# Attention with a mixture of experts behind it: blank rows written as fixed heads of the experts' regions, an expert's last tile placed to end with its tokens, and a smaller descriptor scratch

## The chip, the cores and the metric

One core of a Trainium2 chip. The metric is the device time of one execution in microseconds, the median of several runs.

## The reference

```python
def _attn_ref(q, k, v, w1, b1, w2):            # 8 batches, 8 heads, 576 rows, head_dim 64
    scores = scale * q @ k.T + bias            # bias from a small MLP of relative positions
    attn = softmax(scores)
    return attn @ v

def _moe_ref(x, modality_id, w_gate, modality_bias, w1, w2):   # x: 4608 tokens of 512
    logits = x @ w_gate + modality_bias[modality_id]
    e_idx = np.argmax(logits, axis=1)          # one of 8 experts for each token
    gate_w = softmax(logits) at e_idx
    for e in range(E):
        mask = e_idx == e
        h = np.maximum(x[mask] @ w1[e], 0.0)   # 512 -> 1024
        out[mask] = gate_w[mask, None] * (h @ w2[e])
```

## The kernel before

**Attention.** After a table of biases (up to about 66 us) come 32 pairs of heads, four to a batch, about 17 us each. The order of the work of a pair is written out by hand in `ORDER`, five units of letters: S scores, t and T transposes of the exponentials, a and A, b and c the products with V, 0 to 4 the preparation of Q and K of the next pair, W its swap (two DMAs that write the other half of QT, L426 and L427), K its copies of KH and QD, V its load of V, L the loads of Q and K of the pair after that, q and k their split on GpSimd (L384, L388). The letters X and B are places for routing work: each takes the next step from a list of two kinds in `self.bg` (`route_next`; X takes kind 0, B kind 1). X stands in units 0, 2 and 4, B in units 0, 1 and 2. Routing steps exist from the end of pair 4 on, when the first batch is done; before that `bg` is None and the places are empty.

**Routing.** `route_steps` computes, for each batch, the tokens' experts, counts (`base`, the next free row in each expert's region) and positions, and scatters the rows (token, gate, id) with an indirect DMA of GpSimd (L904) into `xg`, a tensor in HBM: 8 regions of `n_tab` = 4864 rows of 516 words, and 32 rows behind them.

**Experts.** Work goes in tiles of TS = 256 rows of one expert. The first K = 5 tiles (`moe_first`) are made of full tiles known after six of the batches; beside them runs the routing of the last batch. Then come the remaining large tiles (`moe_rest`), and up to NT = 3 tiny tiles of NS = 32 rows for remainders. Tables (`first`, `big`, `tiny`; `table`, `last_tables`) say for each tile which expert it has and at which row of `xg` it starts; VectorE makes them on one partition in some thirty short instructions. A tile is `phase1` (x by w1, L1229) and `phase2` (hidden by w2, L1246, two halves). In the middle of `phase2` stand the transposes of the next tile's rows (`xprep`, L1209), so `load_rows` (L1131, a DMA from `xg` into one of two buffers `gx`) must have landed by then; `load_rows(4)` is issued after tile 2, `load_rows(5)` after tile 3. Weights are loaded on condition that the expert is new (`load_new`, L1122 and L1125), and split into a high and a low part by ScalarE (L1191) and VectorE (L1192), one part of w2 between each two groups of `phase1`, and w1 ahead of `phase2`. All these DMAs are issued by SyncE, in the order of the program.

**Blank rows.** An expert's last tile reads past its tokens. So that what it reads there is harmless (zeros, and the id `n_tok`, which the output's scatter leaves out), `fill_steps` writes blank rows: 32 behind the regions (L1147) and, for each expert, 256 rows from where its tokens end (L1157, the row read from `tab_end`). The steps marked F in the list in `moe_first` issue them, in tiles 2 and 3; each letter string of that list is used up by one call of `beside`, six for a tile. All are writes to `xg`, as the scatters are, at rows known only when the kernel runs; so the framework makes each wait for the one before, and the loads of rows wait for them.

Of the kernel before, what the change touches and what calls it, by code (L numbers as in the profile page):

```python
# [11 lines left out]
F32 = mybir.dt.float32  # L12
BF16 = mybir.dt.bfloat16
F32R = mybir.dt.float32r
I32 = mybir.dt.int32
AF = mybir.ActivationFunctionType
ALU = mybir.AluOpType
AX = mybir.AxisListType
# [3 lines left out]
P = 128  # L22
# [7 lines left out]
E = 8  # L30
# [80 lines left out]
class Attn:  # L111
# [501 lines left out]
    def attention(self):  # L613
        n_pair = self.n_pair
        tail = self.first_tiles() if self.K else {}
        for at in self.ROUTE_LATE:
            tail.setdefault(at, []).append(lambda: next(self.route, None))
        for u, k in self.LATE:
            tail.setdefault((0, u), []).append(lambda k=k: next(self.late[k], None))
        bg = None  # L620
        for n in range(n_pair + 1):
            for u in range(5):
                for f in tail.get((n, u), ()):
                    f()
                if u == 4 and n > 0 and n % NP == 0:
                    assert not bg or all(k == len(x) for x, k in bg)
                    bg = self.route_steps(n // NP - 1)
                m, w = (n, u - 2) if u >= 2 else (n - 1, u + 3)
                scored = []
                for op in self.ORDER[u].split():  # L630
                    op, self.defer = op[0], int(op[1:] or 0)
                    if op in "aAbc":
                        self.flush(lambda x: x[0][0] in "er")
                    elif op in "WK" or (op == "S" and u == 0):
                        self.flush(lambda x: x[0][0] == "p")
                    elif op == "X":
                        self.flush(lambda x: x[0][0] == "a")
                    self.held = [] if self.defer and op in "01234tTRAc" else None
                    if op in "SefC":
                        if n == n_pair:  # L640
                            continue
                        if op == "S":
                            scored.append(self.scores(n, 2 * u + len(scored)))
                        elif op == "C":
                            self.compact(n, u)
                        else:
                            self.exps(*scored["ef".index(op)])
                    elif op in "tT":
                        if 0 <= m < n_pair:
                            self.etrans(m, w, "tT".index(op))  # L650
                    elif op in "RaAbc":
                        if n > 0:
                            self.rtrans(n - 1) if op == "R" else self.av(n - 1, *divmod("aAbc".index(op), 2))
                    elif op in "01234WKV":
                        if n + 1 < n_pair:
                            if op in "01234":
                                self.prep(n + 1, int(op))()
                            else:
                                {"W": lambda: self.swap(n + 1), "K": lambda: self.heads(n + 1), "V": lambda: self.load_v(n + 1)}[op]()
                    elif op in "qkL":  # L660
                        if n + 2 < n_pair:
                            self.load_qk(n + 2) if op == "L" else self.split(n + 2, "qk".index(op))
                    elif f := self.route_next(bg, "XB".index(op)):
                        f()
                    fresh, self.held = self.held or [], None
                    for x in self.waiting:
                        x[2] -= 1
                    self.flush(lambda x: x[2] <= 0)
                    self.waiting += fresh
                if 0 <= m < n_pair:  # L670
                    del self.E[m, w]
        self.flush(lambda x: True)
        self.bg = bg


    def route_setup(self, cp):
# [2 lines left out]
        B = self.B  # L679
        NC = 5 * B  # L680
        self.n_tab = -(-self.n_tok // TS) * TS + TS
        self.xg = self.dp.tile([E * self.n_tab + NS, XW], F32, name="xg")

        self.ones = cp.tile([P, P], BF16, name="ones")
        nc.gpsimd.memset(self.ones, 1.0)
# [12 lines left out]
        self.base = cp.tile([P, E], F32, name="base")  # L698
        nc.sync.dma_start(self.base, io["c_ebase"].to_broadcast([P, E]))
        yield  # L700
        self.gi = cp.tile([P, 5, 4], F32, name="gi")
        nc.gpsimd.memset(self.gi, 0.0)
        self.ids = cp.tile([P, NC], F32, name="ids")
# [227 lines left out]
    def moe_early(self, cp):  # L931
# [12 lines left out]
        self.gk = cp.tile([1, E, self.n_kt], F32, name="gk")  # L944
        self.ge = cp.tile([1, n_tt, E], F32, name="ge")
        self.tf = cp.tile([1, 4, n_tt], F32, name="tabf")
        self.ev = {nm: cp.tile([1, E], F32, name=nm) for nm in ("cnt", "off", "cum", "val", "taken", "start", "big")}
        self.pad = [cp.tile([1, 4 + E], F32, name=f"pad{k}") for k in range(3)]
        for t in self.pad:
            nc.vector.memset(t, 0.0)  # L950
# [3 lines left out]
        nc.vector.memset(self.ev["taken"], 0.0)  # L954
        self.tabs = {nm: cp.tile([1, 4, n], I32, name=f"tab_{nm}") for nm, n in (("first", max(1, self.K)), ("big", hi + 1 - self.K), ("tiny", E))}
        self.idt = cp.tile([P, 4], I32, name="idt")
        self.tab_end = cp.tile([1, E], I32, name="tab_end")
        self.ids_q = [cp.tile([P, 1], I32, name=f"idsq{k}") for k in range(NT)]
        self.quad = cp.tile([P, 1], F32, name="quad")
        nc.sync.dma_start(self.quad, self.io["c_quad"])  # L960
# [51 lines left out]
    def table(self, nm, nt, start):  # L1012
# [10 lines left out]
        def s_cum():  # L1023
            self.running()
            V.tensor_tensor(ev["val"], nt, ev["cum"], op=ALU.subtract)
            V.scalar_tensor_tensor(ev["val"], ev["val"], float(TS), start, op0=ALU.mult, op1=ALU.add)
            V.tensor_tensor(ev["val"], ev["val"], self.eb, op=ALU.add)

        def s_expert():
            V.tensor_tensor(ge, col(tt), row(ev["cum"]), op=ALU.is_ge)  # L1030
# [3 lines left out]

        def s_row():
            V.tensor_tensor(ge, col(f[:, 0, :]), row(self.iota), op=ALU.is_equal)
            V.tensor_tensor(ge, ge, row(ev["val"]), op=ALU.mult)
            V.tensor_reduce(f[:, 1, :], ge, axis=AX.X, op=ALU.add)
            V.scalar_tensor_tensor(f[:, 1, :], tt, float(TS), f[:, 1, :], op0=ALU.mult, op1=ALU.add)
            if nm != "tiny":  # L1040
                V.tensor_tensor(f[:, 1, :], f[:, 1, :], f[:, 3, :], op=ALU.mult)
                return

            empty = float(E * self.n_tab)
            V.scalar_tensor_tensor(f[:, 1, :], f[:, 1, :], -empty, f[:, 3, :], op0=ALU.add, op1=ALU.mult)
            V.tensor_scalar(f[:, 1, :], f[:, 1, :], empty, None, op0=ALU.add)
            V.tensor_copy(tab[:, 0:2, :], f[:, 0:2, :])
            V.tensor_copy(tab[:, 3, :], f[:, 3, :])
# [28 lines left out]
    def last_tables(self):  # L1077
# [2 lines left out]

        def s_count():
            V.tensor_tensor(ev["cnt"], self.base[0:1, :], self.eb, op=ALU.subtract)
            V.tensor_copy(self.tab_end, self.base[0:1, :])
            self.counts(ev["big"], NS + 0.5)
            V.tensor_scalar(ev["start"], ev["big"], float(TS), None, op0=ALU.mult)
            V.tensor_tensor(ev["nt"], ev["cnt"], ev["start"], op=ALU.is_gt)
# [49 lines left out]
    def ids_of(self, t):  # L1136
        return [self.idt[:, (2 * t + w) % 4 : (2 * t + w) % 4 + 1] for w in range(2)]

    def fill_steps(self):

        nc = self.nc
        z = self.lt

        def blank():
            nc.gpsimd.memset(z[:, 0:DM], 0.0)
            nc.gpsimd.memset(z[:, DM:XW], float(self.n_tok))
            nc.sync.dma_start(self.xg[E * self.n_tab : E * self.n_tab + NS, :], z[0:NS, :])  # L1147

        def end(e):
            off = nc.values_load(  # L1150
                self.tab_end[0:1, e : e + 1],
                engines=[mybir.EngineType.SP],
                min_val=0,
                max_val=E * self.n_tab - TS,
                skip_runtime_bounds_check_because="an expert's rows end one tile before the next expert's",
            )
            nc.sync.dma_start(  # L1157
                self.xg[ds(off, TS), :].rearrange("(p w) c -> p w c", w=2),
                z.rearrange("p (o c) -> p o c", o=1).to_broadcast([P, 2, XW]),
            )  # L1160

        return [blank] + [lambda e=e: end(e) for e in range(E)]

    def gate(self, t):
        return [self.gates[:, (2 * t + w) % 4 : (2 * t + w) % 4 + 1] for w in range(2)]
# [157 lines left out]
    def route_rest(self):  # L1323
        while any((f := self.route_next(self.bg, kind)) and [f()] for kind in (1, 0)):
            pass
        for f in self.fills:
            f()

    def moe_first(self):


        steps = iter("B,X,X,X,,X,BB,,X,B,B,X,X,X,X,X,BBF,BBFF,BF,BF,BF,BF,BBF,BF".split(","))

        def beside():
            for op in next(steps, ""):
                f = next(self.fills, None) if op == "F" else self.route_next(self.bg, "XB".index(op))
                if f:
                    f()

        self.fills = iter(self.fill_steps())  # L1340
        if self.K > 1:
            self.load_rows(1)
        if self.K:
            self.moe_load(1)
        for t in range(self.K):
            self.tile(t, beside)
        self.route_rest()
# [164 lines left out]
```

## Time and profile before

| | |
|---|---|
| Time, median of 3 runs | 1101.06 us (1100.25 to 1104.41) |
| The profiled execution's own time | 1102.27 us |
| Its span, first to last instruction | 1100.5 us |
| Busy: TensorE, VectorE, ScalarE, GpSimd | 96%, 69%, 59%, 29% |
| TensorE's granted clock, mean | 0.991 |
| DMA | 128.09 MB, mean 116 GB/s |

The span is cut by stage: biases to about 66 us, attention to about 630, the first five tiles to about 790, the other tiles to the end. Busy shares are means over these stages. The chain of waits goes back from the last instruction to what released it, step by step; a stretch that the chain spends away from TensorE is one in which TensorE waited.

### The profile page before, as it was taken

The numbers are of one execution on the slowest core, as the hardware profiler recorded it, in microseconds if no ns is written. First come the engines' busy times: TensorE is split into PE (matmuls) and PEld (weight loads), VectorE is DVE, ScalarE is ACT, GpSimd is POOL, SyncE is SP. The second block draws the span as 40 slices with busy tenths as digits, with TensorE's granted clock in tenths as the row PEclk, the third lists the DMA queues.
The fourth block names the chain that finished last, engine by engine and source line by source line (L and its number), as shares of the span: only waits on it lengthen the run. The fifth ranks groups of instructions, "written<-read, shape, count | busy, mean of one in ns | idle before, by whom it ended". The sixth has DMA issues, their size and how long they took to land.

```text
span 1100.5 us, 23117 instructions
## 1 busy us (share of the span) xinstructions
PE 1060.9 (96%) x8324; PEld 889.9 (81%) x8324; DVE 761.9 (69%) x1665; ACT 647.6 (59%) x1250; POOL 318.9 (29%) x546
## 2 busy tenths in 40 slices
PE   6979999999999999999999999999999999999994
PEld 3458878888787888888887889988999999889894
DVE  7976678787786877877879776774556654555553
ACT  7766766666666667666666664444555545454552
POOL 0003425535435345273452321521101111101010
PEclk9999999999999999999999999999999999999998
DMA  6984444535354444445353710134113811243310
GB/s 170 225 189 98 124 111 102 155 81 159 96 136 123 114 128 118 119 126 126 102 148 94 228 54 29 69 132 154 50 39 115 296 62 56 84 148 118 113 40 22
DMA packets 88764, 128.09 MB, mean 116 GB/s; under 512 B 30752, under 2 KB 55584, under 8 KB 88642
## 3 DMA queue, kind: packets, MB, share of 16 engines
q1 hardware_dynamic: 82626, 107.58, 35.9%
q0 software_dynamic: 5920, 18.95, 4.8%
q8 instruction: 68, 1.11, 0.4%
q14 instruction: 54, 0.44, 0.1%
q10 hardware_dynamic: 96, 0.00, 0.0%
HBM read 135.62 MB, written 23.44 MB: 145 GB/s over the span
## 4 chain that ended last, share of the span: by engine, by line
PE 81%; DMA 7%; POOL 5%; DVE 4%; issue 1%; ACT 1%; SPq 0%; POOLq 0%; ACTq 0%; DVEq 0%
PE p L1246 16%; PE p L1229 16%; PE xps L545 12%; PE sps L453 11%; PE eps L497 7%; PE xps L402 4%; PE xps L539 3%; PE bps L199 3%; DMA xg<-NBm 3%; POOL qs L384 2%; PE xps L1209 1%; PE eps L503 1%; POOL xg L904 1%; DMA NBm<-xTb 1%; DVE Eb L468 1%
## 5 line engine op out<-in xcount | busy, mean ns | idle before, releaser
L482 ACT ACTIVATE Eb<-Eb,mn 128x576 f32<-128x576 f32 x288 | 222.9, 776 | 145.8 <-DVE mn L468 143.8
L453 PE MATMUL sps<-KT,QT 128*128 128x288 f32 x1152 | 204.6, 312 | 3.7 <-DVE mn L468 2.3
L468 DVE CUSTOM_DVE_ANT_0 Eb<-sps,NBm 128x576 f32<-128x576 f32 x256 | 185.6, 753 | 11.3 <-PE sps L453 4.4
L453 PEld LDWEIGHTS sps<-KT,QT 128*128 128x128 f32 x1152 | 162.0, 188 | 9.3 <-issue 2.9
L1229 PE MATMUL p<-QT,w1hi 128*128 128x256 f32 x1136 | 161.0, 284 | 0.0
L1229 PEld LDWEIGHTS p<-QT,w1hi 128*128 128x128 f32 x1136 | 146.9, 191 | 3.8 <-issue 1.8
L1232 DVE SCALAR_TENSOR_TENSOR hl<-p,hh 128x512 fp32r<-128x512 f32 x72 | 49.7, 690 | 144.3 <-ACT hh L1231 144.3
L497 PE MATMUL eps<-idf,Eb 128*128 128x128 f32 x1024 | 143.8, 275 | 0.0
L545 PE MATMUL xps<-eT,vraw 128*64 128x288 f32 x1024 | 141.8, 412 | 0.5 <-DVE KT L340 0.5
L1255 POOL DMA_INDIRECT out<-mo,idt x36 | 40.9, 1136 | 317.1 <-ACT QT L1212 222.0
L487 POOL COPY rem<-Eb 128x128 f32<-128x128 f32 x128 | 36.6, 293 | 317.2 <-ACT Eb L482 316.6
L338 ACT ACTIVATE eT<-eps 128x512 f32<-128x512 f32 x160 | 94.2, 590 | 41.3 <-PE eps L497 41.2
L497 PEld LDWEIGHTS eps<-idf,Eb 128*128 128x128 f32 x1024 | 113.5, 141 | 6.2 <-DVE mn L468 5.0
L1246 PE MATMUL p<-w2hi,hh 128*128 128x512 f32 x288 | 115.0, 399 | 0.0
L1246 PE MATMUL p<-w2hi,hl 128*128 128x512 f32 x288 | 113.0, 392 | 0.0
L1231 ACT ACTIVATE hh<-p 128x512 fp32r<-128x512 f32 x72 | 43.0, 597 | 116.9 <-PE p L1229 112.9
L545 PEld LDWEIGHTS xps<-eT,vraw 128*64 128x64 f32 x1024 | 65.2, 137 | 48.5 <-issue 12.3
L340 DVE COPY xTb<-xps 128x288 f32<-128x288 f32 x64 | 29.3, 457 | 106.7 <-PE xps L545 58.7
L1192 DVE TENSOR_TENSOR w2lo<-NBm,w2hi 128x1024 fp32r<-128x1024 f32 x72 | 88.2, 1225 | 18.7 <-ACT w2hi L1191 18.7
L1229 PE MATMUL p<-QT,w1lo 128*128 128x256 f32 x568 | 91.3, 283 | 0.0
L1192 DVE TENSOR_TENSOR w1lo<-NBm,w1hi 128x1024 fp32r<-128x1024 f32 x72 | 83.2, 1219 | 7.2 <-ACT w1hi L1191 7.2
L340 DVE COPY eT<-eps 128x512 f32<-128x512 f32 x128 | 84.6, 682 | 0.0
(230 smaller groups left out, 1849.1 us busy)
## 6 DMA issues: line engine op xcount, KB each, us to landing
NBm<-moe_w SPq DMA_DIRECT2D x23, 2048.0 KB
NBm<-moe_w SPq DMA_DIRECT2D x44, 1024.0 KB
QT<-QT SPq DMA_DIRECT2D x64, 304.0 KB
NBr<-xg SPq DMA_DIRECT2D x20, 516.0 KB
NBm<-xTb SPq DMA_DIRECT2D x32, 288.0 KB
KH<-KT SPq DMA_DIRECT2D x64, 144.0 KB
qraw<-q SPq DMA_DIRECT2D x32, 256.0 KB
kraw<-k SPq DMA_DIRECT2D x32, 256.0 KB
```

What stands on the lines that cost most here:

```text
L338: self.nc.scalar.activation(out, ps, AF.Copy, scale=scale)
L340: self.nc.vector.tensor_copy(out, ps)
L402: nc.tensor.transpose(pr[:, j, :], xs[:, 4 * (part % 2) + j, :, :].rearrange("p a d -> p (a d)"), self.idr)
L453: nc.tensor.matmul(ps[:, half, :], q, k[:, HS * half : HS * half + HS], start=i == 0, stop=i == len(terms) - 1, skip_group_check=True,)
L468: nc.vector.tensor_tensor_reduce(out=e.rearrange("p (t w) -> p t w", t=2), in0=ps, in1=nb.rearrange("p (t w) -> p t w", t=2), scale=1.0, s ...
L482: self.nc.scalar.activation(e, e, AF.Exp, bias=mn, scale=-1.0, accum_out=sm)
L497: nc.tensor.transpose(ps[:, k, :], e[:, part, P * k : P * k + P], self.idf)
L545: nc.tensor.matmul(ps[o, :], v[:, h, k, :], self.eT[:, h, k, sl], start=half == 1 and k == 0, stop=half == 0 and k == 3, tile_position=(0, ...
L1192: self.nc.vector.tensor_tensor(l, w, h.bitcast(F32), op=ALU.subtract)
L1229: nc.tensor.matmul(ps[:, a, :], w[:, c, fs], x[:, c, :], start=i == 0, stop=i == len(ops) - 1)
L1232: nc.vector.scalar_tensor_tensor(hl[:, sl, :], ps, 0.0, hh[:, sl, :].bitcast(F32), op0=ALU.max, op1=ALU.subtract)
L1246: nc.tensor.matmul(ps, h[:, f, sl], m[:, f, :], start=i == 0, stop=i == len(ops) - 1)
```

## The change

Each region gets a head: its first 256 rows are written blank at a fixed place, before any token is scattered, by nine DMAs (eight regions and one region more, which stands where the 32 rows behind the regions stood). They take the X places of pairs 1 to 3, and their source is a tile of its own, `blank`, filled by GpSimd in `route_setup`. The writes behind the tokens, `tab_end` and the steps F are gone. The tables `big` and `tiny` get a limit for each expert, max(end of its tokens - width, start of its region), and a tile starts at the lesser of its old row and that limit: the last tile of an expert ends with its tokens and computes some rows a second time, with the same result; a region with fewer tokens than a tile reads into its head. The program's scratch for descriptors of GpSimd's DMAs is set to 2048 bytes in each partition, where nothing was set.

```diff
--- before.py
+++ after.py
@@ -622,6 +622,8 @@
             for u in range(5):
                 for f in tail.get((n, u), ()):
                     f()
+                if n == 1 and u == 0:
+                    bg = self.blanks()
                 if u == 4 and n > 0 and n % NP == 0:
                     assert not bg or all(k == len(x) for x, k in bg)
                     bg = self.route_steps(n // NP - 1)
@@ -679,7 +681,7 @@
         B = self.B
         NC = 5 * B
         self.n_tab = -(-self.n_tok // TS) * TS + TS
-        self.xg = self.dp.tile([E * self.n_tab + NS, XW], F32, name="xg")
+        self.xg = self.dp.tile([(E + 1) * self.n_tab, XW], F32, name="xg")
 
         self.ones = cp.tile([P, P], BF16, name="ones")
         nc.gpsimd.memset(self.ones, 1.0)
@@ -698,6 +700,10 @@
         self.base = cp.tile([P, E], F32, name="base")
         nc.sync.dma_start(self.base, io["c_ebase"].to_broadcast([P, E]))
         yield
+        blank = cp.tile([P, 2, XW], F32, name="blank")
+        nc.gpsimd.memset(blank[:, :, 0:DM], 0.0)
+        nc.gpsimd.memset(blank[:, :, DM:XW], float(self.n_tok))
+        self.blank = blank
         self.gi = cp.tile([P, 5, 4], F32, name="gi")
         nc.gpsimd.memset(self.gi, 0.0)
         self.ids = cp.tile([P, NC], F32, name="ids")
@@ -944,7 +950,7 @@
         self.gk = cp.tile([1, E, self.n_kt], F32, name="gk")
         self.ge = cp.tile([1, n_tt, E], F32, name="ge")
         self.tf = cp.tile([1, 4, n_tt], F32, name="tabf")
-        self.ev = {nm: cp.tile([1, E], F32, name=nm) for nm in ("cnt", "off", "cum", "val", "taken", "start", "big")}
+        self.ev = {nm: cp.tile([1, E], F32, name=nm) for nm in ("cnt", "off", "cum", "val", "taken", "start", "big", "lim")}
         self.pad = [cp.tile([1, 4 + E], F32, name=f"pad{k}") for k in range(3)]
         for t in self.pad:
             nc.vector.memset(t, 0.0)
@@ -954,7 +960,8 @@
         nc.vector.memset(self.ev["taken"], 0.0)
         self.tabs = {nm: cp.tile([1, 4, n], I32, name=f"tab_{nm}") for nm, n in (("first", max(1, self.K)), ("big", hi + 1 - self.K), ("tiny", E))}
         self.idt = cp.tile([P, 4], I32, name="idt")
-        self.tab_end = cp.tile([1, E], I32, name="tab_end")
+        self.gl = cp.tile([1, n_tt, E], F32, name="gl")
+        self.tl = cp.tile([1, n_tt], F32, name="tl")
         self.ids_q = [cp.tile([P, 1], I32, name=f"idsq{k}") for k in range(NT)]
         self.quad = cp.tile([P, 1], F32, name="quad")
         nc.sync.dma_start(self.quad, self.io["c_quad"])
@@ -1025,6 +1032,9 @@
             V.tensor_tensor(ev["val"], nt, ev["cum"], op=ALU.subtract)
             V.scalar_tensor_tensor(ev["val"], ev["val"], float(TS), start, op0=ALU.mult, op1=ALU.add)
             V.tensor_tensor(ev["val"], ev["val"], self.eb, op=ALU.add)
+            if nm != "first":
+                width = NS if nm == "tiny" else TS
+                V.scalar_tensor_tensor(ev["lim"], self.base[0:1, :], -float(width), self.eb, op0=ALU.add, op1=ALU.max)
 
         def s_expert():
             V.tensor_tensor(ge, col(tt), row(ev["cum"]), op=ALU.is_ge)
@@ -1034,9 +1044,15 @@
 
         def s_row():
             V.tensor_tensor(ge, col(f[:, 0, :]), row(self.iota), op=ALU.is_equal)
+            gl, tl = self.gl[:, 0:T, :], self.tl[:, 0:T]
+            if nm != "first":
+                V.tensor_tensor(gl, ge, row(ev["lim"]), op=ALU.mult)
+                V.tensor_reduce(tl, gl, axis=AX.X, op=ALU.add)
             V.tensor_tensor(ge, ge, row(ev["val"]), op=ALU.mult)
             V.tensor_reduce(f[:, 1, :], ge, axis=AX.X, op=ALU.add)
             V.scalar_tensor_tensor(f[:, 1, :], tt, float(TS), f[:, 1, :], op0=ALU.mult, op1=ALU.add)
+            if nm != "first":
+                V.tensor_tensor(f[:, 1, :], f[:, 1, :], tl, op=ALU.min)
             if nm != "tiny":
                 V.tensor_tensor(f[:, 1, :], f[:, 1, :], f[:, 3, :], op=ALU.mult)
                 return
@@ -1080,7 +1096,6 @@
 
         def s_count():
             V.tensor_tensor(ev["cnt"], self.base[0:1, :], self.eb, op=ALU.subtract)
-            V.tensor_copy(self.tab_end, self.base[0:1, :])
             self.counts(ev["big"], NS + 0.5)
             V.tensor_scalar(ev["start"], ev["big"], float(TS), None, op0=ALU.mult)
             V.tensor_tensor(ev["nt"], ev["cnt"], ev["start"], op=ALU.is_gt)
@@ -1136,30 +1151,13 @@
     def ids_of(self, t):
         return [self.idt[:, (2 * t + w) % 4 : (2 * t + w) % 4 + 1] for w in range(2)]
 
-    def fill_steps(self):
-
-        nc = self.nc
-        z = self.lt
-
-        def blank():
-            nc.gpsimd.memset(z[:, 0:DM], 0.0)
-            nc.gpsimd.memset(z[:, DM:XW], float(self.n_tok))
-            nc.sync.dma_start(self.xg[E * self.n_tab : E * self.n_tab + NS, :], z[0:NS, :])
-
-        def end(e):
-            off = nc.values_load(
-                self.tab_end[0:1, e : e + 1],
-                engines=[mybir.EngineType.SP],
-                min_val=0,
-                max_val=E * self.n_tab - TS,
-                skip_runtime_bounds_check_because="an expert's rows end one tile before the next expert's",
-            )
-            nc.sync.dma_start(
-                self.xg[ds(off, TS), :].rearrange("(p w) c -> p w c", w=2),
-                z.rearrange("p (o c) -> p o c", o=1).to_broadcast([P, 2, XW]),
-            )
-
-        return [blank] + [lambda e=e: end(e) for e in range(E)]
+    def blanks(self):
+
+        def head(e):
+            r = e * self.n_tab
+            self.nc.sync.dma_start(self.xg[r : r + TS, :].rearrange("(p w) c -> p w c", w=2), self.blank)
+
+        return [[[(0, lambda e=e: head(e)) for e in range(E + 1)], 0], [[], 0]]
 
     def gate(self, t):
         return [self.gates[:, (2 * t + w) % 4 : (2 * t + w) % 4 + 1] for w in range(2)]
@@ -1323,21 +1321,17 @@
     def route_rest(self):
         while any((f := self.route_next(self.bg, kind)) and [f()] for kind in (1, 0)):
             pass
-        for f in self.fills:
-            f()
 
     def moe_first(self):
 
 
-        steps = iter("B,X,X,X,,X,BB,,X,B,B,X,X,X,X,X,BBF,BBFF,BF,BF,BF,BF,BBF,BF".split(","))
+        steps = iter("B,X,X,X,,X,BB,,X,B,B,X,X,X,X,X,BB,BB,B,B,B,B,BB,B".split(","))
 
         def beside():
             for op in next(steps, ""):
-                f = next(self.fills, None) if op == "F" else self.route_next(self.bg, "XB".index(op))
-                if f:
+                if f := self.route_next(self.bg, "XB".index(op)):
                     f()
 
-        self.fills = iter(self.fill_steps())
         if self.K > 1:
             self.load_rows(1)
         if self.K:
@@ -1496,7 +1490,7 @@
     import concourse.tile as _tile
     from concourse.bass_utils import run_bass_kernel_spmd as _run
 
-    nc = _bacc.Bacc("TRN2", target_bir_lowering=False, num_devices=1)
+    nc = _bacc.Bacc("TRN2", target_bir_lowering=False, num_devices=1, dynamic_dma_scratch_size=2048)
     b, _, s, _ = inputs["q"].shape
     n_tok = b * s
     arrays = {n: np.ascontiguousarray(inputs[n]) for n in _INS}
```

## Rows read from the trace of the kernel before

**Rows 1.** The page's first part: busy time of each engine, share, instructions.

```profile
PE 1060.9 (96%) x8324; PEld 889.9 (81%) x8324; DVE 761.9 (69%) x1665; ACT 647.6 (59%) x1250; POOL 318.9 (29%) x546
```

**Rows 2.** Chain of waits, 721 to 785 us: start, length in us, what.

```profile
721.71 3.51 DMA xg<-NBm
...
728.61 3.92 DMA NBr<-xg
732.55 5.34 DMA xg<-NBm
...
756.17 4.00 DMA NBr<-xg
...
779.60 5.48 PE p L1246 x24
```

**Rows 3.** Table by phase: busy us (instructions) of each engine, granted clock, DMA share, GB/s.

```profile
724.35:740.45 16.10, 13.50 (x58) 11.05 (x57) 11.51 (x30) 6.97 (x9) 1.99 (x5) 0.89 0.46 167
...
751.95:767.90 15.95, 13.33 (x58) 10.97 (x57) 8.65 (x9) 6.97 (x9) 1.87 (x5) 0.89 0.42 143
...
779.40:791.25 11.85, 11.85 (x58) 9.89 (x57) 7.80 (x9) 6.99 (x9) 1.66 (x5) 1.00 0.17 55
```

**Rows 4.** Waits of TensorE, 640 to 840 us: us in all, times, longest.

```profile
PE xps L1209 <- DMA NBr<-xg: 5.2, 2, 2.6
```

**Rows 5.** Waits of SyncE's queue, 600 to 900 us.

```profile
SPq L1147 <- DMA xg<-NBm,pos: 15.0, 1, 15.0
...
SPq L1147 <- POOL NBm L1146: 1.7, 1, 1.7
```

**Rows 6.** SyncE's queue in order of time, 107 and 720 us: start, length, what.

```profile
107.46 0.46 SPq L426 DMA_DIRECT2D QT<-QT  x1
...
720.80 0.38 SPq L1147 DMA_DIRECT2D xg<-NBm  x1
```

**Rows 7.** VectorE in order of time, 704 to 740 us.

```profile
704.10 4.61 DVE L1192 TENSOR_TENSOR w1lo<-NBm,w1hi 128x1024 fp32r<-128x1024 f32 x4
...
725.46 0.67 DVE L1232 SCALAR_TENSOR_TENSOR hl<-p,hh 128x512 fp32r<-128x512 f32 x1
...
737.66 0.32 DVE L1037 TENSOR_TENSOR ge<-ge,val 1x168 f32<-1x168 f32 x1
...
739.33 0.20 DVE L1057 CAST tab_big<-tabf 1x84 int32<-1x84 f32 x1
```

**Rows 8.** ScalarE in order of time, 730 us.

```profile
730.44 3.89 ACT L1191 CAST w1hi<-NBm 128x1024 fp32r<-128x1024 f32 x4 [4.35 <-DMA NBm<-moe_w]
```

**Rows 9.** GpSimd in order of time, its first work after the start.

```profile
70.80 0.29 POOL L487 COPY rem<-Eb 128x128 f32<-128x128 f32 x1 [68.64 <-ACT Eb L482]
```

**Rows 10.** TensorE in order of time, 81 and 114 us.

```profile
81.44 1.03 PE L453 MATMUL sps<-KT,QT 128*128 128x288 f32 x6 [1.39 <-DMA QT<-QT]
...
114.50 1.31 PE L453 MATMUL sps<-KT,QT 128*128 128x288 f32 x8
```

**Rows 11.** Table of two stretches of 3 us during the early pairs.

```profile
78.00:81.00 3.00, 2.05 (x19) 1.81 (x17) 2.50 (x6) 2.40 (x6) 0.29 (x1) 1.00 1.05 235
105.00:108.00 3.00, 3.00 (x26) 2.71 (x28) 2.54 (x7) 1.52 (x4) 0.29 (x1) 1.00 0.03 4
```

**Rows 12.** Tile xg: ns min/median/max of an instruction, first and last start us.

```profile
L904 POOL DMA_INDIRECT xg<-xrb,pos x35: 937/1021/1158, 184.2 to 635.6; - x35
...
DMA to landing us min/median/max: 2.6/3.3/8.1
```

**Rows 13.** GpSimd in order of time, 703 us.

```profile
703.85 5.76 POOL L904 DMA_INDIRECT xg<-NBm,pos  x1 [1.49 <-DMA xg<-NBm,pos]
```

**Rows 14.** The page's groups of instructions: the scatters of output rows.

```profile
L1255 POOL DMA_INDIRECT out<-mo,idt x36 | 40.9, 1136 | 317.1 <-ACT QT L1212 222.0
```

**Rows 15.** Waits of TensorE's weight loads, whole span.

```profile
PEld xps L402 <- POOL qs L384: 3.7, 12, 0.4
```

## What the change should do to the time

> **What bounds the kernel now.** I read the shares first: TensorE is busy for 1060.9 of 1100.5 us [rows 1]. So only a stretch in which TensorE stands still, or runs at its lower clock, can give time back, and there are some 40 us of standing still in all. Next came the chain of waits, to see whether the instructions of the diff are in it. They are: from 721.71 to 760.17 us (756.17 + 4.00) the chain leaves TensorE and runs through eight writes of blank rows, one after the other, the first of 3.51 us and the longest of 5.34, with two loads of a tile's rows between and behind them, at 728.61 and 756.17 [rows 2]. Third, the waits of TensorE in 640 to 840 us: one cause, line 1209 (`xprep`) waiting for the rows, twice, 5.2 us in all [rows 4]. Last, TensorE's table by phase, for what a stop costs beside its own length: a second phase of a tile takes 11.85 us when its rows are there (779.40 to 791.25), but 16.10 and 15.95 us in the two that wait, with a mean granted clock of 0.89 in each [rows 3]. A granted clock under 1 means that for part of the phase the engine ran at 1.2 of its 2.4 GHz; the work is the same in all three, so the difference holds the stop and the clock.
>
> **The change, part by part.**
>
> *Writes taken out of tiles 2 to 4.* The first late load (tile 4's rows, 728.61) stands in SyncE's queue behind the short blank write and two ends; the second (tile 5's rows, 756.17) behind six more [rows 2]. Without them the first has only the last scatter of tokens to wait for. The trace shows when that landed: the short blank write waited 15.0 us for it and then another 1.7 us for GpSimd's memset, and issued at 720.80 [rows 5, 6], so the scatter was down at 720.80 - 1.7 = 719.1. The load then starts there, 9.5 us earlier. It took 3.92 us [rows 2], so it lands near 723, and TensorE asks for it in the middle of the second phase, at 728.61 + 3.92 - 2.6 = 729.9 [rows 2, 4]: 7 us of room. The conditional load of weights behind it in the queue (`load_new(4, 0)`) moves up too, and with it ScalarE's split of w1, which started only at 730.44 after 4.35 us of waiting [rows 8]; it can now start when its engine is free, at 726.1 (730.44 - 4.35).
> The second load then waits for its table instead (`tab_big`, written at 739.33 to 739.53 [rows 7]). That is VectorE work after tile 3's transposes; it moves forward with TensorE by some 4 us and back by what is added to it, under 1 us (below): some 736 to 737. Landing 4.00 us later [rows 2] is 741. TensorE wants it at 757.6 (760.17 - 2.6, [rows 2, 4]), which with the first stop gone is 753.3: 12 us of room. Both stops should go whole, with the low clock behind them: (16.10 - 11.85) + (15.95 - 11.85) = 4.25 + 4.10 = **8.35 us**.
>
> *What is late next.* In the second phase of tile 3 it would be VectorE. Added to the tables of `tiny` and of `big` are four instructions each (the limit, its product, its sum, the minimum), removed is one copy. By the like instructions of the larger table a product is 0.32 us, a sum I take at the same, and an operation on one short row at no more than the copy into the table, 0.20 us [rows 7]: at most 0.20 + 0.32 + 0.32 + 0.20 = 1.04 us for each table, 2.1 us in all, spread over tiles 2 and 3. In tile 3's first phase VectorE has no gap to speak of, so the last `hl` there, done at 725.46 + 0.67 = 726.13 [rows 7], comes up to 1.0 us later, at 727.1. The phase that reads it begins at 724.35 [rows 3] and takes `hh` and `hl` in turn, 24 matmuls in 5.48 us [rows 2], 0.23 each; the last pair's `hl` of that split is the 14th, at 724.35 + 13 x 0.23 = 727.3. So it is just in time: cost 0, at the worst 0.5 us. The w1 split on VectorE follows, after the last w2 split and what is left of the table, at about 729, and takes 4.61 us; with `xl` behind it (two operations of the size of `hl`, 0.67 us each) [rows 7] it ends near 735, and tile 4's first phase begins at 740.45 - 4.25 = 736.2. In time by 1 us.
>
> *Nine heads beside pairs 1 to 3.* Each is 256 rows of 516 words, 516 KB, the size of an end write, and waits for nothing but the memset of its source. Three X places in each pair: units 0, 2 and 4. SyncE issues a transfer in about 0.5 us [rows 6]; no wait is added ahead of what stands behind them in its queue (the loads of V, the copies of KH and QD). The transfers that could hurt are those that TensorE needs soonest: the swap of QT, issued near 107.46 [rows 6] for a pair that begins at 114.50 [rows 10]: 7 us. The head of unit 0 goes out some 3.5 us before the swap, into a stretch in which the DMA engines are 0.03 busy [rows 11], so it is mostly down by then. The other two follow the loads of Q and K, and what comes behind them (V, KH, QD) is wanted a pair later. The cost is bounded below by 0; no gain, since nothing is taken from this stage. Above it is bounded by the one case in which a swap was caught behind a full queue: at 78 to 81 us the DMA share was 1.05 and TensorE stood 1.39 us for QT [rows 10, 11]. Three pairs like that are 4.2 us. I take 0, since the stretch at 105 to 108 us is the nearer row.
>
> *Blank memset.* Two memsets at the very start on GpSimd, which from there has no work for 68.6 us [rows 9]: 0. The first scatter of tokens now waits for the nine heads; it starts at 184.2 [rows 12], long after pair 3, which begins at 114.50 [rows 10], has issued the last of them: 0.
>
> *The last tile moved back.* 18 tiles of 256 rows run (36 output scatters [rows 14]), and 18 x 256 = 4608 is the number of tokens, so at most the 3 x 32 rows of the tiny tiles are computed twice. No tile more, no tile fewer: 0.
>
> *Scratch of 2048 bytes.* The trace shows no use of it. If it were too small, GpSimd's scatters would take longer or wait. From below 0. From above, each scatter would hold GpSimd until the one before it has landed, 3.3 us [rows 12]. I take 0: each scatter into `xg` already waits for the one before it to land (all write one tensor), so there is hardly more than one outstanding. The one long scatter, 5.76 us at 703.85, is no full buffer: VectorE runs four instructions without a break from 704.10 to 708.71 and the scatter ends 0.9 us behind them [rows 7, 13], about what a scatter takes by itself. On this the Trainium skill speaks against the change: Debugging Trainium Hangs, section Descriptor Overflow, names too many descriptors for a scratch of 16 KiB a partition as a cause of hangs, and this leaves an eighth of it. DMA: Bandwidth & Descriptors (The descriptor swizzle) counts 9 descriptors an engine for a transfer of 128 partitions, of 16 bytes each; an estimate from that is 144 bytes of 2048 a scatter, and by it the sum stays. No run here shows it.
>
> **Sum.** 1100.5 - 8.35 = 1092.2 of span. The profiled execution took 1102.27 us, 1.8 over its span and 1.2 over the median of the three runs, 1101.06. From the median: 1101.06 - 8.35 = 1092.7 us.
>
> **The rivals.**
> A. *The heads reach the swaps of pairs 2 to 4.* For it: a full queue did stop TensorE once [rows 10, 11]. Against it: the heads stand where the engines are nearly idle. 1092.7 + 4.2 = 1096.9.
> B. *One of the two stops stays*, since a new wait takes its place: the rows of tile 5 behind a table that VectorE finishes later, or VectorE itself late in tile 3. Against it: 12 us of room for the one, 0.5 to 1 for the other. About 4.2 us of the gain are gone: 1096.9.
> C. *Slower: the small scratch makes GpSimd wait for each scatter.* Place: pairs whose split of Q (line 384) follows a scatter on GpSimd. The split has no room: TensorE's loads already wait for it 12 times, 0.3 us each [rows 15]. So from there each us of a scatter is a us of the kernel: 12 x 3.3 = 40, and 1092.7 + 40 = 1132. It is slower by more than 0.5% (5.5 us) once a scatter takes (5.5 + 8.35) / 12 = 1.2 us longer.
> D. *The change doesn't do what it says*: the loads of rows still wait for late writes to `xg`. Against it: none are left but the scatters. 1101.
>
> **How the numbers follow.** Forecast 0.76, A 0.08, B 0.06, C 0.06, D 0.04. Likeliest 1092.7. The range: the runs of before lie 0.8 under and 3.3 over their median, VectorE may cost 0.5, and A and B reach 1096.9; below, the lowest run and a little of the clock: 1091 to 1097.5. About 0.5% is what a measurement of this kernel can tell from no change, so faster means under 1095.6: the forecast, and a little of A and B, 0.80. Within 0.5% are D and the rest of A and B, 0.13. Slower is C and the unforeseen, 0.07.
>
> **What would show it.** In the profile after: no wait of line 1209 for rows; second phases of tiles 3 and 4 of 11.9 us with clock 1.00; the load of tile 4's rows near 719 and that of tile 5's before 740; no wait of TensorE for QT in pairs 1 to 4; scatters of 1.0 us. I am wrong if TensorE waits in pairs 2 to 4, if scatters grow, or if VectorE becomes the releaser in tile 3.

## The result, and the profile after

The changed kernel takes 1088.03 us (median of four runs, 1086.78 to 1089.5); the kernel before took 1101.9 us (median of four). The ratio is 0.9874, with a 95% interval of 0.9855 to 0.9894: 13.9 us less, where 8.35 were forecast. That is below the low end of the range, 1091 us. The profiled executions stand likewise: a span of 1086.5 us against 1100.5.

The experts' stage first. TensorE's table by phase, same columns as [rows 3], for the second phases of tiles 2, 3 and 4:

```profile
726.02:737.86 11.84, 11.84 (x59) 9.85 (x58) 11.36 (x30) 6.98 (x9) 1.67 (x5) 1.00 0.08 30
749.37:761.17 11.80, 11.80 (x59) 9.84 (x58) 7.66 (x8) 6.99 (x9) 1.65 (x5) 1.00 0.18 61
772.68:784.52 11.84, 11.84 (x59) 9.85 (x58) 7.66 (x8) 6.98 (x9) 1.67 (x5) 1.00 0.20 59
```

All three are alike, at a granted clock of 1.00; in [rows 3] the first two were 16.10 and 15.95 us. The chain of waits, same columns as [rows 2], no longer leaves TensorE in this stretch:

```profile
731.50 0.87 PE xps L1207 x8
732.37 5.49 PE p L1244 x24
737.86 11.51 PE p L1227 x96
749.37 5.47 PE p L1244 x24
754.84 0.87 PE xps L1207 x8
```

SyncE's queue in order of time, with the loads of rows of tiles 4 and 5:

```profile
721.22 0.56 SPq L1146 DMA_DIRECT2D NBr<-xg  x1
723.04 0.07 SPq L1137 DMA_DIRECT2D NBm<-moe_w  x1
...
739.07 0.55 SPq L1146 DMA_DIRECT2D NBr<-xg  x1
```

The distances between the transposes of the next tile's rows (`xprep`) show the gain of this stage. TensorE in order of time, the kernel before, four tiles:

```profile
706.51 1.03 PE L1209 MATMUL xps<-idf,NBr 128*128 128x128 f32 x8
...
732.58 1.97 PE L1209 MATMUL xps<-idf,NBr 128*128 128x128 f32 x8 [2.60 <-DMA NBr<-xg]
...
760.22 1.12 PE L1209 MATMUL xps<-idf,NBr 128*128 128x128 f32 x4 [2.62 <-DMA NBr<-xg]
...
784.91 1.04 PE L1209 MATMUL xps<-idf,NBr 128*128 128x128 f32 x8
```

In the kernel after none of them waits; they begin at 708.02, 731.34, 754.68 and 777.99. From the first to the last are 78.40 us before and 69.97 now, so 8.43 us are gone here.

The rest lies where the forecast had not looked. Behind TensorE's last matmul (done at 1086.44 before) one output scatter follows, and behind that only the closing instructions of the program. The kernel before, GpSimd in order of time, its last instruction:

```profile
1088.08 0.98 POOL L1255 DMA_INDIRECT out<-mo,idt  x1 [4.69 <-ACT mo L1254]
```

Its closing instructions on GpSimd's queue, the increment of a semaphore and three drains, by line (ns min/median/max, first to last start):

```profile
L1376 POOLq INC_SWDGE_SEM  x1: 1764/1764/1764, 1091.1 to 1091.1; - x1
...
L1508 POOLq DRAIN  x3: 40/107/6533, 1093.1 to 1100.2; - x3
```

The same two views of the kernel after:

```profile
1081.19 0.98 POOL L1253 DMA_INDIRECT out<-mo,idt  x1 [4.69 <-ACT mo L1252]
```

```profile
L1370 POOLq INC_SWDGE_SEM  x1: 404/404/404, 1084.1 to 1084.1; - x1
...
L1502 POOLq DRAIN  x3: 40/107/980, 1084.7 to 1086.3; - x3
```

From the start of the last scatter to the end of the span were 12.4 us (1100.5 - 1088.08); now 5.3 (1086.5 - 1081.19). One increment of a semaphore fell by 1.36 us and one drain by 5.55: 6.9 of the 7.1 us. The scatter, and what stands ahead of it, are the same. The chain of waits ends with this scatter in both kernels, so it never shows these microseconds.

The account closes: 8.43 at the two stops and 7.11 at the end are gained. Against that, the profile after reaches TensorE's first transposes of remainders in pair 1 later by 1.27 us (83.58 against 82.31), and takes 0.24 us more from there to tile 2 (624.44 against 624.20). That makes 14.03, against a difference of the spans of 14.0. The 1.27 us at the start vary between executions: in the two profiles below of the old kernel with a smaller scratch, which has no heads, that point stands at 81.91 and at 83.74.

### The profile page after: what moved, and what is told of

It is laid out like the page before. It is cut to its first block, busy times and chain, and to the rows that moved or that the text cites. A ratio compares the mean times of both kernels' runs of the same rounds, so it can differ in the third digit from the quotient of the medians.

```text
span 1086.5 us, 23090 instructions
## 1 busy us (share of the span) xinstructions
PE 1059.5 (98%) x8324; PEld 887.6 (82%) x8324; DVE 762.4 (70%) x1672; ACT 647.7 (60%) x1250; POOL 318.4 (29%) x546
## 4 chain that ended last, share of the span: by engine, by line
PE 85%; POOL 5%; DVE 4%; DMA 2%; issue 2%; ACT 1%; SPq 0%; POOLq 0%; ACTq 0%; DVEq 0%
PE p L1227 18%; PE p L1244 18%; PE xps L545 12%; PE sps L453 11%; PE eps L497 7%; PE xps L402 4%; PE xps L539 3%; PE bps L199 3%; POOL qs L384 2%; PE xps L1207 1%; DVE Eb L468 1%; PE eps L503 1%; POOL xg L910 1%; DMA NBm<-xTb 1%; POOL xrb L906 1%
```

## The experiments

Two questions: is the end of the program owed to the scratch, and were the reasons for the 8.4 us and for the zeros right?

**The scratch by itself.** The kernel before with the last line of the diff alone.

```diff
-    nc = _bacc.Bacc("TRN2", target_bir_lowering=False, num_devices=1)
+    nc = _bacc.Bacc("TRN2", target_bir_lowering=False, num_devices=1, dynamic_dma_scratch_size=2048)
```

> The kernel before with the scratch of 2048 bytes and nothing else of the change. Theory T: the last two instructions of GpSimd that belong to its DMAs take a time in proportion to the scratch. From the two profiles, DRAIN went from 6533 to 980 ns and INC_SWDGE_SEM from 1764 to 404 ns, together 6.9 us. So here they are 980 and 404 ns, from the start of the last output scatter to the end of the span it is 5.3 us instead of 12.4, the time falls by 6.9 us to about 1095.0 (0.9937), and the two stops of TensorE at the rows (5.2 us) stay. Rival R: the shorter end comes from the writes of blank rows that are gone, or from the last tile's place; then the end stays 12.4 us and the time 1101.9.

Measured: 1096.86 us (eight executions, 1094.44 to 1099.33) against 1103.36, ratio 0.9937 (0.9916 to 0.9957). The closing instructions:

```profile
L1508 POOLq DRAIN  x3: 40/107/980, 1091.5 to 1093.0; - x3
```

The drain and the increment (404 ns) are those of the kernel after, and the waits of TensorE for rows are still there (4.5 us in two). So the scratch alone gives some 6.5 us, at the end, and does not take the stops away.

**All but the scratch.** The changed kernel with a large scratch, and the source of the heads cut to one row read twice, since two rows would not fit beside it.

```diff
-        blank = cp.tile([P, 2, XW], F32, name="blank")
+        blank = cp.tile([P, XW], F32, name="blank")
...
-        self.blank = blank
+        self.blank = blank.rearrange("p (o c) -> p o c", o=1).to_broadcast([P, 2, XW])
...
-dynamic_dma_scratch_size=2048)
+dynamic_dma_scratch_size=13312)
```

> The whole change with a scratch of 13312 bytes instead of 2048 (the most that fits beside it; for this the source of the heads is one row of 516 words, read twice). Theory T: the end grows by 11264 x (6.9 / 14336) = 5.4 us against the changed kernel, DRAIN about 5.3 us and INC_SWDGE_SEM about 1.5; time about 1093.4 (0.9923), no wait of TensorE for rows: this is what the forecast of 8.35 us priced. Rival R: 1088, the end 5.3 us as in the changed kernel.

Measured: 1094.42 us against 1103.36, ratio 0.9912 (0.9882 to 0.9942): some 9 us less. No wait for rows; `xprep` at 707.80, 731.12, 754.47 and 777.78, as in the kernel after. The closing instructions are those of the kernel before:

```profile
L1502 POOLq DRAIN  x3: 40/107/6533, 1086.1 to 1093.2; - x3
```

Apart from the source of the heads this is the change as the forecast had priced it, and its 8.35 us lie inside the interval, 6.4 to 13 us. My expectation of the drain was wrong: it is the same to the nanosecond at 13312 bytes as where nothing is set, so it isn't in proportion to the size that is set.

**A scratch of 512 bytes**, again in the kernel before; by rival C this is where GpSimd must wait.

> The kernel before with a scratch of 512 bytes. Theory T: a further 1536 x 0.00048 = 0.7 us against 2048 bytes: DRAIN about 0.39, INC_SWDGE_SEM about 0.26 us, time about 1094.3 (0.9931). Rival C of the forecast (a small scratch makes GpSimd wait): scatters longer than 1.0 us at the median, GpSimd's splits of Q late, TensorE waiting for line 384, up to 40 us slower than before.

Measured: 1099.63 us, ratio 0.9974 (0.9959 to 0.9989). The end is shorter still (drain 327 ns), but more than half of its gain is lost on the way. Waits of TensorE and of its weight loads for the split of Q, over the span (us in all, times, longest), which stood at 3.7 us for the loads in [rows 15]:

```profile
PE xps L402 <- POOL qs L384: 5.3, 12, 1.1
```

```profile
PEld xps L402 <- POOL qs L384: 8.1, 12, 1.4
```

The scatters last no longer (median 1026 ns against 1021 in [rows 12]); the idle time of GpSimd ahead of one is 0.52 us instead of 0.28 (medians of the 35). From pair 1 to tile 2 the kernel takes 628.48 us instead of 624.20. So rival C's mechanism exists, in rival C's place, but at 0.24 us a scatter; the 3.3 us that I gave it as a bound are not seen.

**Size or use?** The kernel before with its scratch as it was and only the last 2 of GpSimd's 79 DMAs. It doesn't compute the reference's result and is there for its closing instructions alone.

```diff
-                nc.gpsimd.indirect_dma_start(
-                    out=self.xg,
-                    out_offset=IndirectOffsetOnAxis(ap=st["pos"][0:n, c : c + 1], axis=0),
...
+                nc.sync.dma_start(self.xg[r : r + n, :], xr[0:n, :])
...
+        if not getattr(self, "put", False):
+            return
```

> The kernel before, its scratch as it was, with only the last two of GpSimd's 79 DMAs left: tokens go to xg by plain DMAs in their own order, tiles read fixed rows, only the last tile writes its output. What the kernel computes is not the reference's; it is there for the last instructions of GpSimd alone. By the scratch's size (theory T as it stands): DRAIN 6.5 us, INC_SWDGE_SEM 1.76, as before. By its use (theory U: what was written into it since the start, up to its size): DRAIN under 0.5 us, INC_SWDGE_SEM under 0.4.

Measured, the closing instructions of one execution:

```profile
L1510 POOLq DRAIN  x3: 40/107/245, 1079.5 to 1081.2; - x3
```

With the full scratch and two DMAs the drain is 245 ns and the increment 231. So it is use that costs, not size by itself; that a small scratch limits how much use can pile up fits the next table, but is argued and not shown. The figures fit a count: 6533 is 80 times 81.7 ns, one for each of the 79 DMAs and one more; 245 is 3 times that, for two DMAs and one more.

**The dose.** The changed kernel with 1024, 4096 and 8192 bytes.

> The changed kernel with a scratch of 1024 bytes. From 2048 and 512 bytes: DRAIN between 980 and 327 ns, about 0.55 us, INC_SWDGE_SEM about 0.30; the end 0.5 us shorter. If the wait of 0.24 us that 512 bytes put ahead of each scatter is there too, the pairs with scatters grow by up to 3.7 us in all and the kernel is at 1091; if it comes only below 1024, 1087.5, the same as the changed kernel within what can be measured.

> The changed kernel with a scratch of 4096 bytes in place of 2048. GpSimd's last drain took 80 units of 81.7 ns where 79 DMAs fitted (6533 ns), 3 units after two DMAs (245 ns), 4, 8 and 12 units at 512, 1024 and 2048 bytes (327, 653, 980 ns). Theory U (the end costs one unit for each DMA whose descriptors have not been taken back, so it grows with the scratch until all 79 fit): 20 to 28 units at 4096, a drain of 1.6 to 2.3 us and an increment of 0.55 to 0.75 us, the end 0.8 to 1.7 us longer than in the changed kernel; the waits of TensorE for line 384's split fall from 1.0 us to 0.2, some 0.2 to 0.8 us back; time within 0.15% of the changed kernel's 1088.0, ratio 0.986 to 0.989. Rival (the end is one constant below some size and another above it): a drain of 0.98 us again, or of 6.53 us and then a time near 1094.

> The changed kernel with a scratch of 8192 bytes. By theory U 40 to 64 units: a drain of 3.3 to 5.2 us and an increment of 1.0 to 1.45 us, the span some 3 to 5.3 us longer than in the changed kernel, 1089.5 to 1092. By the rival the drain is 0.98 or 6.53 us.

Measured, with the sizes from above; the units are drains divided by 81.7 ns, and the idle time of GpSimd is the median ahead of the 35 scatters of the routing:

| scratch, bytes | increment, drain, ns | units | idle ahead of a scatter, us | TensorE waits for line 384 | ratio to before |
|---|---|---|---|---|---|
| not set | 1764, 6533 | 80 | 0.28 | 0.2 (1) | 1 |
| 13312 (changed) | 1764, 6533 | 80 | 0.28 | 0.2 (1) | 0.9912 |
| 8192 (changed) | 704, 2205 | 27 | 0.28 | 0.2 (1) | one run, 1089.76 us |
| 4096 (changed) | 404, 980 | 12 | 0.28 | 0.2 (1) | 0.9866 (0.9849 to 0.9882) |
| 2048 (changed) | 404, 980 | 12 | 0.28, two of 0.61 | 1.0 (3) | 0.9874 (0.9855 to 0.9894) |
| 1024 (changed) | 324, 653 | 8 | 0.52 | 4.4 (10) | 0.9882 (0.9866 to 0.9899) |
| 512 (before) | 244, 327 | 4 | 0.52 | 5.3 (12) | 0.9974 (0.9959 to 0.9989) |

At 1024 bytes the wait of 512 bytes is there too, as one of the two expected ways had it. Two of my expectations fell: at 4096 bytes I expected 20 to 28 units and at 8192 at least 40; there are 12 and 27. The rival, one constant below a size and another above it, falls by the 27. Every drain is a whole number of units, and the number grows with the scratch or stays, but what sets it between 512 and 8192 bytes is open. Of the sizes tried 4096 stands best in the trace: the drain of 2048, and no wait of TensorE for the split beyond those of before (624.20 us from pair 1 to tile 2, as before, against 624.44 at 2048). In time the two can't be told apart.

**The late writes put back.** The changed kernel, with its scratch, and the nine writes of before issued again at their old places, first from the new source:

```diff
...
+            nc.sync.dma_start(self.xg[ds(off, TS), :].rearrange("(p w) c -> p w c", w=2), self.blank)
...
-        steps = iter("B,X,X,X,,X,BB,,X,B,B,X,X,X,X,X,BB,BB,B,B,B,B,BB,B".split(","))
+        steps = iter("B,X,X,X,,X,BB,,X,B,B,X,X,X,X,X,BBF,BBFF,BF,BF,BF,BF,BBF,BF".split(","))
```

> The changed kernel with the nine late writes of blank rows put back into tiles 2 and 3, heads and tables and the scratch of 2048 bytes kept. Theory T: the late writes cost the two stops with their low clock, 8.4 us, wherever the rest stands; second phases of tiles 3 and 4 of 16 us again, time 1088.0 + 8.4 = 1096.4 (0.9950 of the kernel before), and the same as before with only the small scratch (1096.9), since heads and table instructions cost nothing. Rival A of the forecast (heads reach the swaps): up to 4 us slower than that, 1100, and TensorE waiting for QT in pairs 2 to 4.

Measured: 1091.54 us, ratio 0.9885 (0.9869 to 0.9902); I had expected 1096.4. The stops came back, but short. Chain of waits:

```profile
743.29 3.12 DMA xg<-blank
746.42 2.66 DMA xg<-blank
749.22 4.57 DMA xg<-blank
753.93 3.92 DMA NBr<-xg
757.89 1.09 PE xps L1229 x8
```

Waits of TensorE, 640 to 840 us:

```profile
PE xps L1229 <- DMA NBr<-xg: 2.2, 2, 1.4
```

The edit had restored the order, not the source: `blank` holds two rows side by side, where before one row was read twice. So I restored that too:

```diff
-            nc.sync.dma_start(self.xg[ds(off, TS), :].rearrange("(p w) c -> p w c", w=2), self.blank)
+            nc.sync.dma_start(
+                self.xg[ds(off, TS), :].rearrange("(p w) c -> p w c", w=2),
+                self.blank[:, 0:1, :].to_broadcast([P, 2, XW]),
+            )
```

> The changed kernel (scratch 2048, heads, tables as changed) with the nine late writes back in tiles 2 and 3 at their old places in SyncE's queue, and with the source that they had before: one row of 516 words a partition, read twice. The run with these writes from two rows side by side in SBUF had shown writes of 2.6 to 3.2 us and two stops of which the longest was 1.4 us. Theory S (the form of the source makes the writes longer, and their length makes the stops): writes of 3.3 to 3.8 us again, two waits of line 1207 for rows near 2.6 us each, granted clock under 1 in both second phases, these near 16 us, the three distances between the transposes of the next tile's rows 8 us longer than in the changed kernel; time 1095 to 1097, ratio near 0.994. Rival R (what is shorter is something else, as the 1.7 us of the memset that is no longer waited for): writes no longer than from two rows, stops under 1.5 us, time near 1091.5, ratio 0.989.

Measured: 1097.22 us, ratio 0.9954 (0.9938 to 0.9971). Chain of waits:

```profile
738.23 4.08 DMA xg<-blank
742.32 3.39 DMA xg<-blank
745.73 3.49 DMA xg<-blank
749.23 3.40 DMA xg<-blank
752.76 3.72 DMA xg<-blank
756.62 4.01 DMA NBr<-xg
```

Table of this kernel, 720 to 768 us, columns as in [rows 3]; and its waits of TensorE, 640 to 840 us:

```profile
720.00:736.00 16.00, 13.40 (x86) 11.89 (x85) 12.33 (x33) 9.02 (x12) 2.65 (x6) 1.00 0.47 166
736.00:752.00 16.00, 16.00 (x118) 15.19 (x117) 8.98 (x23) 6.32 (x11) 3.04 (x6) 1.00 0.47 174
752.00:768.00 16.00, 12.66 (x49) 10.22 (x48) 9.10 (x10) 6.87 (x9) 1.86 (x5) 0.79 0.42 133
```

```profile
PE xps L1232 <- DMA NBr<-xg: 5.9, 2, 3.3
```

With the old source the writes last 3.4 to 4.5 us, the stops are those of before and a little more, the clock falls behind the second, and the `xprep` distances sum to 79.06 us, 9.1 more than in the kernel after. So the late writes in SyncE's queue are the cause of the 8.4 us, and most of it hangs on the form of their source, which leaves 2.6 us (72.59 - 69.97) or 9.1: the two kernels differ in hardware-queue packets by 1024 (83922 against 82898), that is 128 for each of eight writes, which fits one packet a partition of two rows instead of two of one row. This kernel can't be told from the old one with the small scratch alone (0.9937, 0.9916 to 0.9957), so heads and tables together cost nothing that these intervals show.

The length of a stop does not tell whether the clock falls. In this run the first stop, 2.60 us, left the granted clock at 1.00, and the second, 3.34 us, was followed by the lower level; in the kernel before two stops of 2.60 and 2.62 us were each followed by it. In the run with 512 bytes two longer ones were not: the clock stays at 1.00 from 716 to 772 us, and the transposes behind them take 1.09 us, where at the lower clock they took 1.97:

```profile
738.94 1.09 PE L1209 MATMUL xps<-idf,NBr 128*128 128x128 f32 x8 [3.25 <-DMA NBr<-xg]
...
766.26 1.09 PE L1209 MATMUL xps<-idf,NBr 128*128 128x128 f32 x8 [3.30 <-DMA NBr<-xg]
```

**Heads made four times as heavy**, to see whether rival A can be reached: four writes of 256 rows in each of the nine places.

```diff
-            r = e * self.n_tab
-            self.nc.sync.dma_start(self.xg[r : r + TS, :].rearrange("(p w) c -> p w c", w=2), self.blank)
+            for j in range(4):
+                r = e * self.n_tab + TS * j
+                self.nc.sync.dma_start(self.xg[r : r + TS, :].rearrange("(p w) c -> p w c", w=2), self.blank)
```

> The changed kernel with four writes of 256 rows at each of the nine places instead of one (the first 1024 rows of each region; 36 writes, 19 MB in 54 us). If one head at a place is far from the limit, this costs little: the two writes' places behind the loads of Q and K have a pair's room, and only unit 0's four (4 x 1.4 us of DMA time, ahead of the swap by 3.5 us) can reach it: 0 to 2 us for each of three pairs, at most 6 us, 1088 to 1094. If a single head already stood at the limit (rival A), four would add 3 x 4 us of waits for QT and more for Q, K and V: over 1100.

Measured: 1107.71 us, ratio 1.0037 (1.0022 to 1.0052), far above the 1088 to 1094 that I had expected. Waits of TensorE, whole span, and the table of pair 4's stretch:

```profile
PE sps L453 <- DMA QT<-QT: 15.6, 4, 7.3
```

```profile
117.00:134.00 17.00, 10.14 (x67) 8.74 (x68) 4.22 (x11) 5.67 (x14) 6.90 (x9) 0.80 0.95 325
```

The same stretch of the kernel after:

```profile
117.00:134.00 17.00, 17.00 (x142) 14.23 (x141) 11.73 (x29) 11.41 (x27) 7.89 (x13) 1.00 0.69 208
```

With one head a place the DMA share is 0.58 to 0.74 between 84 and 151 us (0.43 to 0.52 before) and TensorE never stops; with four it is 0.82 to 0.95, TensorE stands 15.6 us for the swaps of QT, and its clock falls. The cost isn't proportional to the bytes: one head a place costs nothing that the trace shows, four cost some 18 us by the two ratios. Where between the two it begins was not tried.

## Why the prediction was right and wrong

*The step that failed is the scratch*, as the prediction put it: "The trace shows no use of it", "From below 0", "I take 0". It bounded this edit from above only, by rival C, and gave no reason that excluded a gain; there was one of 6.9 us. Its reason for 0, that hardly more than one scatter is outstanding, spoke of transfers in flight, while the drain of before fits a count of all 79 DMAs, among them 35 that began 450 us and more ahead of it [rows 12]. That term is what carries the time out of the range: the sum with it is 1092.7 - 6.9 = 1085.8, and the 2.2 us from there to 1088.03 are less than the 4.2 us by which runs of the kernel before differ. The trace of before did show the use of the scratch, two instructions of 1764 and 6533 ns on GpSimd's queue behind the last scatter. I said "some 40 us of standing still in all" and never asked where they are: 14 of them (1086.44 to 1100.5) lie behind the last matmul, and the chain of waits, which I read for them, ends at 1089. The low end of the range held nothing but the lowest run and a little of the clock.

*The two stops* were right in mechanism, and in size for these two profiles: 8.43 us against 8.35. The load of tile 4's rows was forecast at 719.1 and came at 721.22, in a profile whose marks all lie 1.5 us later here; that of tile 5's was to wait for its table until 736 to 737, and waited 9.2 us for `tab_big` to issue at 739.07. The prediction said that a stop costs more than its own length and took the price from the phases themselves. That price is one of this execution, not of a stop in general: before, two stops of 2.6 us cost 8.4 us, with the clock at its lower level for a part; with 512 bytes two of 3.25 and 3.30 us cost 7.5 (`xprep` from 712.22 to 789.66 us, 77.44 against 69.97), at full clock; two of 0.7 and 1.4 us, in the run with the late writes from two rows, cost 0.9 and 1.7 (distances of 24.20 and 24.99 instead of 23.3), at full clock. So the agreement to 0.1 us is in part luck.

*VectorE in time* was right. Its new instructions take 0.15 + 0.32 + 0.32 + 0.17 = 0.96 us for the larger table and 0.83 for the smaller (forecast at most 1.04 each). TensorE has no wait for it in tile 3, and the last `xl` is done at 735.6, 2.3 us before the first phase of tile 4; 1 us was forecast.

*Heads, memset, last tile moved back: 0*, all right. TensorE's one wait for QT is 0.9 us, in pair 1, where [rows 10] had 1.39. The heavier heads show that rival A was a real mechanism with room left: the bound from one caught swap, 4.2 us for three pairs, would have been far too low for four heads a place.

*Rival C* was right in place and mechanism, wrong in price. At 512 and 1024 bytes GpSimd does wait, 0.24 us ahead of most scatters, and TensorE's wait for the split grows to 5.3 and 4.4 us; at 2048 two scatters of 35 show it (0.61 us). The 1.2 us from which it would have decided was not reached at any size. The Trainium skill, Debugging Trainium Hangs (Descriptor Overflow), names an overflowing scratch of 16 KiB as a cause of hangs: here 79 DMAs ran through with 2048, 1024 and 512 bytes, and what showed was a wait.

## What to carry to other kernels

Before pricing a change, lay out all the idle time of the bounding engine by stretch, the part behind its last instruction included: the chain of waits may end short of the span's end, and what a chain doesn't show can still be gained. A setting of which one can say only that the trace shows no use of it needs a bound on both sides; look on the queue of the engine that owns it, up to the last instruction. And when undoing one part of a change, undo its operands too: an order restored with another source brought back less than a third of the effect.

## What the runs showed of the hardware

- The end of a program with indirect DMAs of GpSimd costs time behind the last of them: an increment and a drain of 1.76 and 6.53 us after 79 DMAs with the scratch as it comes, 0.23 and 0.25 us after two. A scratch of 4096 or 2048 bytes makes it 0.40 and 0.98 us; at 1024 and 512 most scatters of the routing wait 0.24 us more.
- A write of 516 KB from two rows side by side in a partition took 2.6 to 3.2 us in six of eight cases (4.6 and 5.0 in the others), from one row read twice 3.4 to 3.8 in six of eight (4.1 and 4.5), with twice the packets.
- Stops of TensorE of 2.60, 2.62 and 3.34 us were followed by a stretch at the lower clock; others of 2.60, 3.25 and 3.30 us, and the one of 1.4 us, left the granted clock at 1.00.
